# Turning the keys by VectorE and device memory instead of TensorE, in a gated linear attention with a squared-ReLU feed-forward

## The chip, the cores and the metric

One core of one Trainium2 chip runs the whole kernel in one launch. The metric is device time in microseconds (us) of that launch. The kernel before took 495.83 us, the median of three runs (495.6 to 496.37).

## What is computed

All inputs are float32. For 4 sequences (B), 8 heads (H), 768 steps (S) and head dimension 48 (D):

```
f = sigmoid(f_logit)
for t in range(S):
    state = f[:, :, t, :, None] * state + k[:, :, t] (outer) v[:, :, t]
    y[:, :, t] = q[:, :, t] @ state
x = y as [B*S, 384]
out = relu(x @ w_in)**2 @ w_out        # w_in [384, 2048], w_out [2048, 384]
```

The recurrence is a gated linear attention; the feed-forward part holds nearly all the multiplications.

## The kernel before, in words

**Blocks and units.** The 768 steps are cut into 6 blocks of 128 steps (TB). A block of one pair of heads is a *unit*: 24 units, four in each block. A unit works in two chunks of 64 steps (C). Units of head pairs 0 to 2 (`own`) load gates, keys and queries (`fkq`, transposed: head rows on the partitions, 4 x 128 steps along them) and values (`vn`, steps on the partitions). 112 of their 128 rows belong to the pair itself (ROWS); the 16 last rows of either half belong to head pair 3, which has no load of its own: its keys and queries are gathered from the three other units into `last_kq` (stage `m`, L469), its turned keys into `last_kn`.

**The stages of a unit** are letters (L626 to L651): `L` and `v` load; `G` is the sigmoid on ScalarE; `K` (L445) scans the gates on VectorE and multiplies them into the keys (`kt`); `Q` (L458) does the same for the queries; `T` (L494) turns the keys with four 128x128 transposes on TensorE into the PSUM tile `pk`; `N` (L502) copies them on ScalarE to `kn` (steps on the partitions) and to `last_kn`; `D` (L517) multiplies `kn` with the values to the update of the state and `S` the keys with the queries to the scores, both into the PSUM pair `ds`; `M` masks the scores, `C` updates the states, `r` and `s` copy halves, `Y` (L566) computes the outputs, `H` and `X` split them into a high and a low part, the feed-forward's `x`; `h` and `g` send the rows of head pair 3 to the other tiles of `x` by DMA.

**The feed-forward part** works in *rounds*, one for each 128 of the 2048 hidden columns: `up` (9 matmuls of 128x512 into one of two PSUM banks in turn, L247), `square` (ScalarE: relu, square, a copy `gh`, L257 to L259), `rest` (VectorE: `gl`, the remainder, L264), and `down` of the round two earlier (9 matmuls into `po`, L274). The bank of a round is free for the round two later when `rest` has read it. I number the rounds from 0 on: block 1 has rounds 0 to 15, the second half of block 0 has 16 to 23 (its first half is done in an opening part written out by hand, FIRST and SECOND), and blocks 2 to 5 have 24 to 39, 40 to 55, 56 to 71 and 72 to 87. In the first round of a block stands the last `down` of the block before and its output (`finish`, L333, copies and DMAs on SP); the second round of a block has no `down`, so it is only half as long.

**Order.** Every engine works through its instructions in the order in which the program issues them, SP its DMAs too, and a DMA that waits holds up those behind it. Units of blocks 2 to 5 are hung on rounds by hand. Each unit has a *slot*, a round (SLOTS, L63: 12, 14, 18, 20 for block 2; 22, 28, 31, 34 for block 3; 37, 44, 47, 50 for block 4; 53, 60, 63, 66 for block 5; of each four, the last is head pair 3's). In its slot, after `rest`, the stages `Y` of the unit before, then its own `D` and `S`, `H X` of the one before, `r M C`, `m` are issued (L793). Stages ahead of the slot are in STAGE_AT (L60) as (rounds before the slot, place in that round, letters): place 0 is ahead of `up`, 0.5 between `square` and `rest`, 0.7 behind `rest`, 1 behind `down`:

```
STAGE_AT = ((-5, 0, "Lv"), (-3, 1, "GK"), (-2, 0.5, "Q"), (-1, 1, "TN"))
```

So `K` stands at the end of the third round before the slot, `Q` in the next round ahead of its `rest`, and `T` at the end of the round before the slot. `fkq` has a ring of three buffers, `kn` has one.

Of the kernel before, what the change touches and what calls it, by code (L numbers as in the profile page):

```python
# [12 lines left out]
F32 = mybir.dt.float32  # L13
# [10 lines left out]
P = 128  # L24
B, H, S, D = 4, 8, 768, 48
DM, DFF = 384, 2048
HP = H // 2
C = 64
TB = 128
NBLK = S // TB  # L30
NC = TB // C
NT = B * TB
NZ = B * NC
CZ = C + 1
ROWS = 64 + D
# [14 lines left out]
NBUF = 3  # L50
HEADS = 4

# [1 line left out]

STAGE_AT = ((-5, 0, "Lv"), (-3, 1, "GK"), (-2, 0.5, "Q"), (-1, 1, "TN"))  # L60
LAST_AT = ((-5, 0, "v"),)

SLOTS = (12, 14, 18, 20, 22, 28, 31, 34, 37, 44, 47, 50, 53, 60, 63, 66, 69)  # L63
# [297 lines left out]
def fast_path(ctx, tc, moe, ident, low, fkqT, vN, w, w4, out):  # L361
    nc = tc.nc
    V, G = nc.vector, nc.gpsimd
    pers = ctx.enter_context(tc.tile_pool(name="pers", bufs=1))
    dr = pers.tile([P, NZ * CZ], F32, name="dr")
    dz = pers.tile([P, NZ * CZ], F32, name="dz")
    mask = pers.tile([P, C], F32, name="mask")
# [7 lines left out]
    last_kn = pers.tile([P, B, P], F32, name="last_kn")  # L375
# [7 lines left out]
    for r in (0, C):  # L383
        G.affine_select(
            out=mask[r : r + C], in_=mask[r : r + C], compare_op=ALU.is_ge, fill=0.0,
# [12 lines left out]
    def weights_load(f, i, mark=False):  # L398
        raw = moe.words(f, i)
        if mark:  # L400

            V.memset(raw[0:1, 0:1], 0)
        nc.sync.dma_start(raw, w[f, i].bitcast(I16)[:, 1:])

    class Unit:
# [96 lines left out]
        def turned(self):  # L502
# [5 lines left out]
                in_=self.pk.rearrange("p b (h r) -> p b h r", h=2)[:, :, :, D:],  # L508
            )

        @cached_property
        def ds(self):
            return self.pair("ds", -1)
# [112 lines left out]
        def stage(self, letters):  # L626
            for c in letters:
                {
                    "L": lambda: self.load(slice(0, 3)),
                    "f": lambda: self.load(slice(0, 1)),  # L630
                    "p": lambda: self.load(slice(1, 2)),
                    "z": lambda: self.load(slice(2, 3)),
                    "v": lambda: self.load_v(),
                    "G": lambda: self.gates(),
                    "K": lambda: self.keys(),
                    "Q": lambda: self.queries(),
                    "m": lambda: self.move(),
                    "r": lambda: self.crossed(),
                    "T": lambda: self.turn(),
                    "N": lambda: self.turned(),  # L640
                    "D": lambda: self.add(),
                    "S": lambda: self.scores(),
                    "M": lambda: self.masked(),
                    "C": lambda: self.states(),
                    "s": lambda: self.crossed_states(),
                    "Y": lambda: self.outputs(),
                    "H": lambda: self.upper(),
                    "X": lambda: self.lower(),
                    "g": lambda: self.parts((1,), G if self.blk < 2 else nc.sync),
                    "h": lambda: self.parts((0,), nc.sync),  # L650
                }[c]()  # L651
# [73 lines left out]
    with tc.manual_schedule(engines={ET.PE, ET.SP, ET.DVE, ET.Activation, ET.Pool}):  # L725
        with tc.tile_pool(name="ps_p", bufs=2, space=bass.MemoryType.PSUM) as ps_p:
            for t in FIRST.split():
                step(t)
        moe.psum(ctx, "ps_h1", "ps_o")

        moe.sums_of()
        for t in SECOND.split():
            step(t)
        part = []
        owed = moe.ending(lambda po: part.extend(moe.keep(po)))
        whole = half[0] + half[1]
        order = [(1, whole), (0, half[1])] + [(blk, whole) for blk in range(2, NBLK)]
        hooks = [{} for _ in order]

        def hook(k, n, at, do):  # L740
            while n >= len(order[k][1]):
                k, n = k + 1, n - len(order[k][1])
            hooks[k].setdefault((max(n, 0), at), []).append(do)

        def third():
            early.close()
            moe.inputs(ctx)
            xs[2] = moe.new_x(2, 2)

        halves = [(f, i) for f in half[1] for i in range(2)]
        steps = {}

        def advance(h):
            if h not in steps:
                steps[h] = moe.decode(moe.row[halves[h]], lambda: moe.parts(*halves[h]))
            next(steps[h], None)

        for n in range(1, NF - 1):  # L760
            few = range(3 * (n - 1) // 2, min(3 * n // 2, len(halves)))
            for h in few:
                if n < AHEAD:
                    weights_load(*halves[h])
                else:
                    hook(0, n - AHEAD, 0.5, lambda h=h: weights_load(*halves[h], mark=True))

            def before(few=few):
                for h, last in zip(few, (None, *few)):
                    for m in (h, h, last):  # L770
                        if m is not None:
                            advance(m)

            def after(few=few[:-1]):
                for h in few:
                    advance(h)

            def last(few=few):
                for h in few[-1:]:
                    advance(h)  # L780
                    advance(h)


            for place, do in zip((0, 0.5, 0.7) if n > 1 else (0.7, 0.7, 0.7), (before, after, last)):
                hook(0, n, place, do)
        hook(0, 12, 0, third)
        later = [Unit(n, xs, (ps_a,)) for n in range(2 * HP, NBLK * HP)]
        for un, last, at in zip((*later, None), (None, *later), SLOTS):
            if un:
                for n, place, stage in STAGE_AT if un.own else LAST_AT:  # L790
                    hook(0, at + n, place, lambda un=un, stage=stage: un.stage(stage))

            def slot(un=un, last=last):  # L793
                for who, stage in (last, "Y"), (un, "DS"), (last, "HX"), (un, "rMC"), (un, "m" * bool(un and un.own)):
                    if who:
                        who.stage(stage)
                if last and not last.own:
                    last.stage("hg")

            hook(0, at, 0.7, slot)  # L800
            if un:
                hook(0, at + 1, 0, lambda un=un: un.stage("s"))

        for n in range(2 * NF):
            hook(2 + n // NF, n % NF + SIZES_AT, 1, lambda n=n: moe.sizes(n // 2, n % 2))
        general = []
        found = verdict(nc, moe, low, ident, ps_a)
        for n in range(2):
            hook(len(order) - 2, VERDICT_AT + n, 1, lambda: general.append(next(found)))
        hook(  # L810
            len(order) - 1, VERDICT_AT, 1,
            lambda: general.append(nc.values_load(general[1][0:1, 0:1], min_val=0, max_val=1)),
        )
        for k, (blk, fs) in enumerate(order):
            if blk > 1 and blk + 1 < NBLK:
                xs[blk + 1] = moe.new_x(blk + 1, (0, 1, 2)[blk - 2])
            moe.begin(blk, xs[blk], fs)
            if blk == NBLK - 1:

                moe.third_bank = ps_a  # L820
                obs = moe.third_of("ob_last")
                moe.run(hooks[k], obs, owed)
                moe.third_bank = None
            else:
                moe.run(hooks[k], None, owed)
                owed = moe.ending(
                    lambda po, blk=blk: moe.finish(
                        lambda e: out[blk, e * P : (e + 1) * P], None if blk else part, po, blk
                    )
                )  # L830
# [122 lines left out]
@with_exitstack  # L953
def tile_kernel(ctx: ExitStack, tc: tile.TileContext, fkqT, vN, w, w4, out):
    nc = tc.nc
    const = ctx.enter_context(tc.tile_pool(name="const", bufs=1))
    ident = const.tile([P, P], F32, name="ident")
    low = const.tile([P, NBLK * NJ, B * NC], F32, name="low")
    sums = const.tile([P, 2 * NF], F32, name="sums")
    moe = Moe(ctx, tc, const, sums, out)  # L960
    moe.hidden(ctx)
    with ExitStack() as fast:
        rv, obs = fast_path(fast, tc, moe, ident, low, fkqT, vN, w, w4, out)


    with tc.If(rv > 0):
        with ExitStack() as gen:
            general_path(gen, tc, moe, ident, fkqT, vN, w, out)
        for e in range(NJ):
            nc.sync.dma_start(obs[e], out[NBLK - 1, e * P : (e + 1) * P])  # L970

    for e in range(NJ):
        for n, cs in tails(e):

            (nc.sync if n else nc.scalar).dma_start(out[NBLK - 1, e * P : (e + 1) * P, cs], obs[e][:, cs])
# [61 lines left out]
```

## Time and profile before

| | |
|---|---|
| median of three runs | 495.83 us |
| the profiled execution: its time, its span in the trace | 495.6 us, 493.9 us |
| TensorE, granted clock | full speed (0.999) |
| VectorE, ScalarE busy | 48%, 59% of the span |
| DMA: moved, mean rate | 41.96 MB, 85 GB/s |

The span is what the trace covers; 1.7 us of launch lie around it. A row of the trace names the line, the engine, the tiles as out<-in, the count, and then times. PE is TensorE, DVE VectorE, ACT ScalarE, POOL GpSimd, and SP the engine that issues most DMAs.

### The profile page before, as it was taken

Reading aid. Unit: us, or ns where it says so; the run is one execution under the profiler, and the core shown is the slowest. Engines: PE = TensorE matmul, PEld = TensorE weight load, DVE = VectorE, ACT = ScalarE, POOL = GpSimd, SP = SyncE. Lnnn points to the kernel's source line nnn. Section 1 sums busy time; section 2 is a strip of 40 time slices with the busy share of each in tenths; the row PEclk is TensorE's granted clock in tenths of the full one; section 3 lists DMA queues with packets and bytes.
Section 4 is the critical chain, followed back from the end, with each engine's and each line's share of the span. In section 5 each row is a group of like instructions: output and inputs, shape, how many; then the busy total and the mean of one; then the engine's idle time right before and its main releaser. Section 6 shows DMA issues by size and latency. Waiting matters only on the chain.

```text
span 493.9 us, 11450 instructions
## 1 busy us (share of the span) xinstructions
PE 476.2 (96%) x4815; PEld 383.6 (78%) x4815; DVE 237.1 (48%) x444; ACT 292.4 (59%) x615; POOL 29.6 (6%) x66
## 2 busy tenths in 40 slices
PE   3889999999999999999999999999999999999996
PEld 2767777888888888888888888888888877888884
DVE  7999962657654633553632463541563322211112
ACT  5588875977546554656664766664765543544441
POOL 5422010000000000000000000000000000000000
PEclk9999999999999999999999999999999999999999
DMA  8888106570404025330022411014410002100001
GB/s 290 260 290 283 22 20 238 171 264 17 115 3 155 1 40 157 102 90 1 3 44 94 158 30 65 1 17 109 147 26 12 1 1 34 66 0 1 0 1 69
DMA packets 20588, 41.96 MB, mean 85 GB/s; under 512 B 2752, under 2 KB 6192, under 8 KB 20528
## 3 DMA queue, kind: packets, MB, share of 16 engines
q1 hardware_dynamic: 19936, 40.09, 26.1%
q0 software_dynamic: 448, 0.92, 0.9%
q8 instruction: 40, 0.66, 0.5%
q14 instruction: 20, 0.16, 0.1%
q10 hardware_dynamic: 144, 0.13, 0.1%
HBM read 31.68 MB, written 4.72 MB: 74 GB/s over the span
## 4 chain that ended last, share of the span: by engine, by line
PE 92%; DVE 3%; ACT 1%; DMA 1%; issue 1%; POOL 0%; DVEq 0%; ACTq 0%
PE ph L247 41%; PE po L274 41%; PE ds L533 2%; PE ds L522 2%; PE py L581 2%; PE pk L498 1%; PE ph L581 1%; DVE fkq L448 1%; PE py L593 1%; PE ph L593 1%; DMA x<-ys 1%; DMA fkq<-in_fkqT_dram 1%; DVE fkq L462 1%; DVE fkq L454 0%; PE first_py L581 0%
## 5 line engine op out<-in xcount | busy, mean ns | idle before, releaser
L247 PE MATMUL ph<-x,w 128*128 128x512 f32 x864 | 219.1, 399 | 1.3 <-DVE sc L540 1.2
L247 PEld LDWEIGHTS ph<-x,w 128*128 128x128 f32 x864 | 160.8, 188 | 40.4 <-ACT w L143 1.6
L274 PE MATMUL po<-gh,w 128*128 128x512 f32 x576 | 180.9, 395 | 0.0
L264 DVE TENSOR_TENSOR gl<-ph,gh 128x512 fp32r<-128x512 f32 x96 | 66.3, 691 | 235.0 <-ACT gh L259 235.0
L257 ACT ACTIVATE ph<-ph 128x512 f32<-128x512 f32 x96 | 56.0, 583 | 141.3 <-PE ph L247 141.2
L274 PEld LDWEIGHTS po<-gh,w 128*128 128x128 f32 x576 | 108.3, 188 | 25.0
L274 PE MATMUL po<-gl,w 128*128 128x512 f32 x288 | 115.9, 402 | 0.0
L274 PEld LDWEIGHTS po<-gl,w 128*128 128x128 f32 x288 | 54.1, 188 | 14.0 <-DVE gl L264 0.7
L259 ACT CAST gh<-ph 128x512 fp32r<-128x512 f32 x96 | 56.4, 587 | 3.0
L258 ACT ACTIVATE ph<-ph 128x512 f32<-128x512 f32 x96 | 55.9, 582 | 3.0
L453 POOL TENSOR_SCALAR fkq<-fkq 128x8 f32<-128x8 f32 x18 | 12.3, 685 | 302.2 <-DVE fkq L448 104.5
L492 ACT COPY sx<-sp 48x208 f32<-48x208 f32 x44 | 16.0, 365 | 17.1 <-DVE sp L555 16.3
L448 DVE TENSOR_TENSOR_SCAN fkq<-fz,dr 128x520 f32<-128x520 f32 x18 | 22.2, 1234 | 1.8 <-ACT fz L443 1.7
L462 DVE TENSOR_TENSOR_SCAN fkq<-fz,dz 128x520 f32<-128x520 f32 x18 | 22.3, 1242 | 0.6
L581 PEld LDWEIGHTS py<-sc,vn 64*48 64x48 f32 (+1 forms) x384 | 16.4, 126 | 7.4 <-issue 6.6
L498 PE MATMUL pk<-ident,fkq 128*128 128x128 f32 x72 | 12.3, 299 | 9.2 <-POOL fkq L453 6.2
L581 PE MATMUL py<-sc,vn 64*48 64x64 f32 (+1 forms) x384 | 20.9, 222 | 0.0
L131 ACT CAST head<-raw 128x384 f16<-128x384 bf16 (+1 forms) x33 | 19.6, 628 | 0.3 <-DMA raw<-in_w_dram 0.2
L593 PE MATMUL py<-rx,sx 48*48 48x64 f32 x192 | 19.6, 216 | 0.0
L145 DVE TENSOR_TENSOR w<-wa,w 128x384 fp32r<-128x384 f32 (+1 forms) x33 | 18.0, 548 | 2.0 <-ACT w L143 1.5
L143 ACT CAST w<-wa 128x384 fp32r<-128x384 f32 (+1 forms) x33 | 16.5, 510 | 3.6 <-DVE wa L134 3.4
L498 PEld LDWEIGHTS pk<-ident,fkq 128*128 128x128 f32 x72 | 9.5, 153 | 11.4 <-issue 9.1
(102 smaller groups left out, 470.8 us busy)
## 6 DMA issues: line engine op xcount, KB each, us to landing
raw<-in_w_dram SPq DMA_DIRECT2D x32, 383.8 KB, 5.7
fkq<-in_fkqT_dram SPq DMA_DIRECT2D x15, 768.0 KB, 5.0
vn<-in_vN_dram SPq DMA_DIRECT2D x24, 192.0 KB, 4.8
out_dram<-ob SPq DMA_DIRECT2D x12, 256.0 KB, 2.3
fkq<-in_fkqT_dram SPq DMA_DIRECT2D x9, 256.0 KB, 5.0
x<-ys SPq DMA_DIRECT2D x30, 64.0 KB, 2.4
last_kq<-fkq SPq DMA_DIRECT2D x28, 64.5 KB, 2.3
out_dram<-part SPq DMA_DIRECT2D x3, 256.0 KB, 2.1
```

Of the source, the lines that this page charges most:

```text
L131: nc.scalar.copy(out=self.upper(head, F16), in_=high)
L247: self.nc.tensor.matmul(self.ph[f], lhsT=w[:, i], rhs=x[:, j], start=first and n == 0, stop=last and n == 2)
L257: nc.scalar.activation(ph, ph, AF.Relu)
L258: nc.scalar.activation(ph, ph, AF.Square)
L259: nc.scalar.copy(out=gh, in_=ph)
L264: self.nc.vector.tensor_tensor(out=gl, in0=self.ph.pop(f), in1=gh.bitcast(F32), op=ALU.subtract)
L274: self.nc.tensor.matmul(po[e], lhsT=l, rhs=r, start=f == fs[0] and i == 0, stop=f == fs[-1] and i == 2,)
L448: V.tensor_tensor_scan(out=rr[:, ::-1], data0=self.fz[:, NZ * CZ : 0 : -1], data1=dr[:, ::-1], initial=0.0, op0=ALU.mult, op1=ALU.add,)
L462: V.tensor_tensor_scan(out=pp, data0=self.fz[:, : NZ * CZ], data1=dz, initial=0.0, op0=ALU.mult, op1=ALU.add)
L498: nc.tensor.transpose(out=self.pk[:, b], in_=self.kt[:, b * TB : (b + 1) * TB], identity=ident)
L581: nc.tensor.matmul(self.py[c][h * C : h * C + m, b * C : (b + 1) * C], lhsT=self.vn[rows, b, h * D : h * D + m], rhs=self.sc[rows, h, b], ...
L593: nc.tensor.matmul(self.py[c][h * C : h * C + m, b * C : (b + 1) * C], lhsT=s[rows, b * D : b * D + m], rhs=q[rows], start=False, stop=b = ...
```

## The change

In the units of head pairs 0 to 2 of blocks 2 to 5, twelve in all, `T` and `N` are gone. New stages are `t` (`squares`): one VectorE transpose of 32x32 squares, taking every fourth step, into the spent gate rows of the unit's `fkq`, and a DMA of 256 KB to device memory, in which the steps then lie in order; `b` (`back`): four DMAs from there into `kn`, by runs of 32 or 16 floats (128 or 64 bytes); and `l` (`last_back`): two DMAs of 64-byte runs into `last_kn`, in the slot behind `m`. `G`, `K` and `Q` stand one round earlier. The opening part's units keep `T` and `N`. The diff, with blank lines left out:

```
+SQ = 32
-STAGE_AT = ((-5, 0, "Lv"), (-3, 1, "GK"), (-2, 0.5, "Q"), (-1, 1, "TN"))
+STAGE_AT = ((-5, 0, "Lv"), (-4, 1, "GK"), (-3, 0.5, "Q"), (-3, 0.7, "t"), (-2, 1, "b"))
...
+    aside = ctx.enter_context(tc.tile_pool(name="aside", bufs=1, space=bass.MemoryType.DRAM))
...
+        def squares(self):
+            tr = self.rr[:, :NT].rearrange("p (n b d) -> p n b d", b=B, d=SQ)
+            V.transpose(
+                out=tr.rearrange("p n b d -> p b n d"),
+                in_=self.kt.rearrange("p (b t n) -> p b n t", b=B, n=TB // SQ),
+            )
+            self.steps = aside.tile([P // SQ, TB, B, SQ], F32, tag=f"steps{self.nm}", name=f"steps{self.nm}")
+            nc.sync.dma_start(
+                self.steps.rearrange("g (t n) b d -> (g t) (n b d)", t=SQ), tr.rearrange("p n b d -> p (n b d)")
+            )
+        def back(self):
+            self.kn = self.wk([P, B, ROWS], "kn")
+            for g in range(P // SQ):
+                r, m = g * SQ, min(SQ, ROWS - g * SQ)
+                nc.sync.dma_start(self.kn[:, :, r : r + m], self.steps[g, :, :, :m])
+        def last_back(self):
+            for h in range(2):
+                at = h * C + self.hp * (C - D)
+                nc.sync.dma_start(last_kn[:, :, at : at + C - D], self.steps[2 * h + 1, :, :, D - SQ :])
...
+                    "t": lambda: self.squares(),
+                    "b": lambda: self.back(),
+                    "l": lambda: self.last_back(),
...
-                for who, stage in (last, "Y"), (un, "DS"), (last, "HX"), (un, "rMC"), (un, "m" * bool(un and un.own)):
+                for who, stage in (last, "Y"), (un, "DS"), (last, "HX"), (un, "rMC"), (un, "ml" * bool(un and un.own)):
```

## Rows read from the trace of the kernel before

**Rows 1.** The page of the profile: busy time of each engine, and the chain that ended last, its shares by engine.

```profile
PE 476.2 (96%) x4815; PEld 383.6 (78%) x4815; DVE 237.1 (48%) x444; ACT 292.4 (59%) x615; POOL 29.6 (6%) x66
...
PE 92%; DVE 3%; ACT 1%; DMA 1%; issue 1%; POOL 0%; DVEq 0%; ACTq 0%
```

**Rows 2.** The chain that ended last, in order of time, from 160 to 182 us: start, length, engine, tile, line, count. The `up` of rounds 19, 20, 21 and 22 (round 20 is the slot of a unit of head pair 3, without a turn), and the turn at the end of round 21.

```profile
160.33 2.11 PE ph L247 x9
...
164.54 2.10 PE ph L247 x9
...
171.04 2.11 PE ph L247 x9
...
175.24 0.44 PE pk L498 x4
175.68 2.11 PE ph L247 x9
```

**Rows 3.** All that writes or reads the tile `pk`, from 70 us on (the twelve units in question): count, shortest/median/longest in ns, first and last start.

```profile
L498 PE MATMUL pk<-ident,fkq x48: 271/272/273, 123.6 to 373.5; 128*128 128x128 f32 x48
L504 ACT COPY kn<-pk x12: 532/532/539, 124.2 to 373.8; 128x448 f32<-128x448 f32 x12
L506 ACT COPY last_kn<-pk x12: 270/271/281, 124.6 to 374.2; 128x128 f32<-128x128 f32 x12
```

**Rows 4.** The page's costliest groups: two VectorE operations, of 512 and of 384 elements on a partition, with busy time, mean ns of one, and idle time before them.

```profile
L264 DVE TENSOR_TENSOR gl<-ph,gh 128x512 fp32r<-128x512 f32 x96 | 66.3, 691 | 235.0 <-ACT gh L259 235.0
...
L145 DVE TENSOR_TENSOR w<-wa,w 128x384 fp32r<-128x384 f32 (+1 forms) x33 | 18.0, 548 | 2.0 <-ACT w L143 1.5
```

**Rows 5.** VectorE's instructions in order of time in rounds 24 to 26 (start us, length us): the end of block 0 in round 24 (L339), the `rest` of round 25, `K`'s scan (L448), and the `rest` of round 26 behind `K` and `Q`.

```profile
193.00 1.88 DVE L339 TENSOR_TENSOR part<-po,part 128x512 f32<-128x512 f32 x3
196.59 0.69 DVE L264 TENSOR_TENSOR gl<-ph,gh 128x512 fp32r<-128x512 f32 x1 [1.72 <-ACT gh L259]
197.20 1.23 DVE L448 TENSOR_TENSOR_SCAN fkq<-fz,dr 128x520 f32<-128x520 f32 x1
...
201.42 0.68 DVE L264 TENSOR_TENSOR gl<-ph,gh 128x512 fp32r<-128x512 f32 x1
```

**Rows 6.** The chain from 196 to 212 us: the `up` of round 27, and the beginning of `D` in slot 28.

```profile
198.91 2.10 PE ph L247 x9
...
206.74 0.38 PE ds L522 x23
```

**Rows 7.** ScalarE, and below it VectorE, in rounds 40 and 41, the first of block 3 (start, length): the output copies of block 2 (L342), the sigmoid `G` (L443) and the `rest` of round 41.

```profile
269.74 1.08 ACT L342 COPY ob<-po 128x512 f32<-128x512 f32 x2
...
273.94 0.64 ACT L443 ACTIVATE fz<-fkq 128x512 f32<-128x512 f32 x1
...
274.07 0.69 DVE L264 TENSOR_TENSOR gl<-ph,gh 128x512 fp32r<-128x512 f32 x1 [2.91 <-ACT gh L259]
```

**Rows 8.** The page's list of DMAs: KB of one, and the median us from its issue to its landing.

```profile
fkq<-in_fkqT_dram SPq DMA_DIRECT2D x15, 768.0 KB, 5.0
vn<-in_vN_dram SPq DMA_DIRECT2D x24, 192.0 KB, 4.8
out_dram<-ob SPq DMA_DIRECT2D x12, 256.0 KB, 2.3
```

**Rows 9.** DMA packets in three stretches, one queue of each: packets, MB, and the share of 16 engines' time that they took. From 423 to 430 us (7 us; three outputs, together 384 packets of 2 KB and 48 small ones that signal the ends), from 485 to 494 us (9 us; one output on a queue of its own, 128 packets of 1 KB and 16 small ones), and from 80 to 84 us (4 us; weights, 416 packets of 3 KB and 59 small ones).

```profile
q1 hardware_dynamic: 432, 0.79, 29.3%
...
q10 hardware_dynamic: 144, 0.13, 4.9%
...
q1 hardware_dynamic: 475, 1.28, 85.5%
```

**Rows 10.** SP's DMAs in order of time (start, length of the issues, line, out<-in, count): the outputs of block 1 in round 16; the end of block 0 in round 24, and behind it the loads for slot 31; in round 40's place the load for slot 47.

```profile
151.50 1.65 SPq L343 DMA_DIRECT2D out_dram<-ob  x3
...
193.71 1.53 SPq L343 DMA_DIRECT2D out_dram<-part  x3
195.29 0.60 SPq L436 DMA_DIRECT2D fkq<-in_fkqT_dram  x1
195.94 0.62 SPq L440 DMA_DIRECT2D vn<-in_vN_dram  x1
...
272.06 0.61 SPq L436 DMA_DIRECT2D fkq<-in_fkqT_dram  x1
```

**Rows 11.** The chain from 125 to 380 us: where TensorE begins `D` in slots 12, 18, 31 and 44.

```profile
126.28 0.53 PE ds L522 x23
...
157.10 0.35 PE ds L522 x22
...
221.98 0.38 PE ds L522 x22
...
284.22 0.38 PE ds L522 x23
```

**Rows 12.** VectorE in order of time: the `rest` of round 8; the `rest` of round 28; and the end of stage `C` in slot 28.

```profile
110.92 0.69 DVE L264 TENSOR_TENSOR gl<-ph,gh 128x512 fp32r<-128x512 f32 x1 [1.44 <-ACT gh L259]
...
207.53 0.69 DVE L264 TENSOR_TENSOR gl<-ph,gh 128x512 fp32r<-128x512 f32 x1 [3.94 <-ACT gh L259]
...
210.57 0.35 DVE L560 TENSOR_TENSOR state<-sp,ds 112x192 f32<-112x192 f32 x1
```

## The prediction, made before the changed kernel was run

> **What bounds the kernel now.** I read the page's busy times first, then the chain that ended last. TensorE is busy 96% of the span and makes up 92% of the chain [rows 1]; VectorE at 48% and ScalarE at 59% are not the bound. Next I read the chain in order of time, where TensorE's rounds follow each other without a gap. A round without a turn lasts 164.54 - 160.33 = 4.21 us, a round with one 175.68 - 171.04 = 4.64, and the turn's own piece is 0.44 [rows 2]. So whatever leaves TensorE's queue is gained at full length, and whatever makes TensorE wait is lost at full length. The sum has to be made from waits that do not exist yet.
>
> **What is removed.** Twelve turns, 48 transposes [rows 3]: 12 x 0.44 = 5.3 us of the chain. ScalarE loses 24 copies, 12 x (0.53 + 0.27) = 9.6 us [rows 3]; nothing waits for ScalarE on the chain, so I count them as nothing.
>
> **The transpose on VectorE.** The trace has none. Its nearest row is an operation of 512 elements on a partition, 0.69 us; below stands the one of 384 elements, 0.55 [rows 4]; above, twice 0.69, if each square passed twice. I take 0.69 because the count of elements is the same. Twelve are 8 us on an engine that idles half the time; only their place in the way to `kn` matters.
>
> **K and Q one round earlier.** `Q` stands ahead of its round's `rest`, and `up` two rounds later needs the bank that `rest` frees. In a full round that costs nothing: `Q` delays `rest` by some 2 us, and the bank is wanted nearly 4 us after `rest` would end. But for slots 28, 44 and 60 `Q` moves from the third round of a block into the second, which has no `down`. In the kernel before, from the start of `K` to the end of the `rest` behind `Q` are 201.42 + 0.68 - 197.20 = 4.90 us [rows 5]. For slot 28 `K` can now begin when VectorE has finished block 0, at 193.00 + 1.88 = 194.88 [rows 5]; the `rest` of round 25 then ends at 199.78 instead of 197.28, and `up` of round 27 wants to begin at 198.91 [rows 6]: TensorE waits 0.9 us. For slots 44 and 60 `K` waits for ScalarE's two copies and the sigmoid, 269.74 + 1.08 + 0.64 = 271.5 [rows 7], and `rest` ends at 276.4. In round 25 `up` two rounds later came 198.91 - 196.59 = 2.32 us after the start of the old `rest` [rows 5, 6]; here that is 274.07 + 2.32 = 276.4 [rows 7]. Cost 0. Loss by this step: 0.9 us.
>
> **The way to `kn`.** The write is like an output of 256 KB, 2.3 us from issue to landing [rows 8]; `back` may only issue after that. Its four DMAs bring 128 x 4 runs each, 2,048 packets, 128 on each of 16 engines. No packet of data as short as 128 bytes is in the trace. From the shares of engine time, a packet of 2 KB took 0.293 x 16 x 7 us / 384 = 85 ns, one of 1 KB 0.049 x 16 x 9 / 128 = 55, one of 3 KB 0.855 x 16 x 4 / 416 = 132 [rows 9], the small ones counted in. A line through 1 and 2 KB gives 29 ns for 128 bytes; one through 2 and 3 KB falls below the price by bytes alone, 85 / 16 = 5 ns. I take 16, about midway, so 2.05 us for the four DMAs, and keep 5 and 55 (no dearer than 1 KB) as the ends. SP's issue is 0.6 us for each [rows 10], 2.4 for the four.
>
> Three slots have a load queued between write and `back`: the loads for slots 31, 47 and 63 stand behind `t` of slots 28, 44 and 60. Before, they went out at 195.29 and 272.06, as soon as the block's outputs were out [rows 10]; now SP waits at the write for VectorE. Slot 28: the transpose ends at 199.78 + 0.7 = 200.45, SP issues the write (about 0.35) and then the load at 200.8. The load lands 5.0 us later [rows 8], its values some 0.5 behind (8 packets an engine), at 206.3, and the runs for `kn` queue behind them: 208.35. TensorE wants `D` at 206.74 - 0.44 + 0.9 = 207.2 [rows 6]. **Late by 1.15 us.** Slot 44: transpose at 277.05, load at 277.4, `kn` at 277.4 + 5.5 + 2.05 = 284.95, `D` wanted at 284.22 - 0.44 = 283.8 [rows 11]: late by 1.15, and slot 60 is its twin. Slot 18: `back` stands on SP behind block 1's outputs, the last of them issued near 152.8 and landed at 155.1 [rows 8, 10]; `kn` at 157.2, `D` at 157.10 - 0.44 = 156.66 [rows 11]: late by 0.6. Loss: 4.05 us.
>
> The other eight are on time. Slot 31 as an example: `rest` and the slot's own VectorE work end at 210.92 [rows 12]. Even if the later load puts that off to 214.4, the transpose ends at 215.1, the write lands at 217.4, and four issues and a landing of 2.3 end at 221.5; `D`, wanted at 221.98 - 0.44 [rows 11], has by then moved 2 us back by the waits in slot 28. Slot 12: behind the `rest` of round 8 (110.92 [rows 12]) `K`, `Q`, the weights' steps, a `rest` and the transpose take about 7 us, the write lands near 121, `kn` near 125; `D` is wanted at 126.28 - 0.44 [rows 11].
>
> The loads behind `t` also make ScalarE wait for `G` of the next unit, up to 1.7 us (206 against 204); its next work, the square of the slot's round, is not there before 206.5, which hides it. `l` adds 24 issues behind each `m`, needed one slot later, and the sends to the other tiles of `x` follow much later: nothing. The bytes, 12 x 544 KB = 6.5 MB, meet empty queues except where named.
>
> **Sum.** 495.6 - 5.3 + 0.9 + 4.05 = 495.3 us against the profiled execution's own time; the median of the runs stands 0.2 above that, so **495.5 us**. What a measurement of this kernel can tell from no change is about 0.2%, 1 us. One ns more or less for a short packet is 0.128 x 4 = 0.5 us, so the sign hangs on that price.
>
> **Rivals.**
>
> *The short runs are cheap, and the turns are a gain.* At 5 ns for a packet the four DMAs are bound by SP's issues; `kn` of slot 28 is there at 207.0, slots 44 and 60 alike, slot 18 is 0.1 late. Sum 495.6 - 5.3 + 0.9 + 0.1 = 491.3, by the median 491.5; at 10 ns 492.6. For it speaks that one engine's short signalling packets do not show in the 2 KB price; against it the line from 1 KB. [...]
>
> *The return trip becomes the new wait, and the kernel is slower.* Place: the first `D` of slots 18, 28, 44 and 60. It decides from 17 ns a packet on, where the losses eat the 5.3 us. At 29 ns the four DMAs last 3.7 us: slot 18 is 2.1 late, slots 28, 44 and 60 2.8 each, slot 12 about 0.5. Sum 495.6 - 5.3 + 0.9 + 11 = 502.2, by the median 502.4. For it speaks the row of 1 KB; against it that two queues shared the engines there.
>
> *A run below some size costs as a much longer one.* At the line's 40 ns for 512 bytes the DMAs last 5.1 us: four slots about 4 late, slots 12 and 14 about 2 each, three more 0.5: 21 us, 513 us. At 55 ns it is past 525. [...]
>
> A transpose of twice 0.69 us would move slots 28, 44 and 60 by 0.7 each, 2.1 us: inside the forecast's neighbourhood.
>
> **Chances.** Forecast (494.2 to 497.2 its own range) 36%: 22 within 0.2%, 7 on either side. Cheap runs 32%, all faster. Wait at some 29 ns 22%, a dearer run 10%, all slower. So faster 39%, the same 22%, slower 39%. The range leaves out the dear runs and some of either flank: 491.4 to 503.
>
> **What would show it.** `pk` with 24 transposes instead of 72, TensorE's gain 0.44 for each missing one. One VectorE transpose of about 0.7 us in each of twelve units. A wait of `up` for `rest` (L264) of 0.9 us in round 27, none in rounds 43 and 59. Waits of `D` (L522) for the DMAs into `kn`: about 1.15 us in slots 28, 44, 60, 0.6 in slot 18, none elsewhere. Engine time of a packet into `kn` near 16 ns. Wrong would be: no such waits (cheap runs), waits in most of the twelve slots (dear runs), or a wait on another engine that I have hidden, ScalarE's `G` above all.

## The result, and the profile after

The changed kernel takes 500.73 us (median of 4 runs, 500.28 to 501.0) against 495.83 (4 runs, not the three given further up, 495.6 to 496.37): a ratio of 1.0096, with [1.0079, 1.0114] as its 95% interval. The forecast was 495.5, the same; the kernel is slower by 4.9 us, and the interval lies clear of no change. The profiled execution has a span of 498.7 us against 493.9.

The page of the profile after, busy times and the chain by engine:

```profile
PE 475.9 (95%) x4767; PEld 380.6 (76%) x4767; DVE 249.1 (50%) x456; ACT 284.5 (57%) x591; POOL 29.7 (6%) x66
...
PE 78%; DVE 7%; DMA 6%; ACT 4%; issue 2%; SPq 1%; POOL 1%; POOLq 0%; DVEq 0%; ACTq 0%
```

The 48 transposes and 24 copies are gone, as said. What is new stands in the chain: against [rows 1] TensorE fell from 92% to 78%, and VectorE, the DMAs and ScalarE took most of that share. Waits from 72 us on (us in total, times, longest; PEld is TensorE's loading of weights, so one wait can show on both):

```profile
ACT fz L446 <- DMA fkq<-in_fkqT_dram: 11.9, 5, 2.7
...
PEld ph L249 <- DVE x L641: 2.8, 3, 1.1
...
PE ds L548 <- DMA kn<-steps: 2.4, 6, 0.6
PEld ph L249 <- DVE gl L266: 2.0, 3, 1.3
PE ph L249 <- DVE x L641: 1.4, 2, 0.7
...
PE ph L249 <- DVE gl L266: 0.8, 1, 0.8
```

The wait of `up` for `rest` (L266) and that of `D` (L548) for `kn` were forecast. So was ScalarE's `G` (L446) waiting for loads, but as hidden and up to 1.7 us; it came five times, up to 2.7 us (three times behind `t` as named, twice behind the `back` of slots 14 and 18; these two stay in e1 below, where the loss is gone). The wait of `up` (L249) for `X` (L641) was not forecast.

**Where the time goes, round by round.** For each round I take the start of its first `up` matmul in the changed trace less that in the trace of before, and how much this difference grows from the round ahead of it. In rounds that the change doesn't touch it grows by 0.00 to 0.01 us, so small terms can be read. (Executions of one kernel spread by 3 us and more, before as well: 494.8 to 497.8 beside e9. So the mechanisms below are read from rounds, and only the verdicts from the medians. The time ahead of round 0 is not in the table: it differs by -0.62 to +0.87 us between these traces, where the kernels are the same.)

| kernel | a slot's turn gone | 15 | 19 | 27 | 29 | 45 | 61 | all rounds |
|---|---|---|---|---|---|---|---|---|
| after | -0.36 | 0.21 | 1.22 | 0.99 | 1.66 | 1.84 | 1.49 | 4.61 |
| e1 loads first | -0.36 | 0.05 | 1.32 | 0.99 | 0.05 | 0.16 | 0.23 | -0.38 |
| e2 Q behind rest | -0.36 | 0.58 | 1.18 | 0.00 | 1.87 | 3.51 | 1.68 | 5.60 |
| e3 no turn | -0.36 | -0.09 | 0.36 | 0.00 | -0.09 | -0.09 | -0.08 | -4.82 |
| e4 shift alone | 0 | 0.00 | 0.00 | 0.99 | 0.33 | 0.33 | 0.33 | 2.86 |
| e5 all mends | -0.36 | 0.18 | 0.52 | 0.00 | 1.06 | 1.12 | 1.09 | 0.38 |
| e6 back first | -0.36 | 0.08 | 0.43 | 0.99 | 1.52 | 1.94 | 1.80 | 4.16 |
| e7 Q behind slot | -0.36 | 0.28 | 1.42 | 0.99 | 0.95 | 1.06 | 1.14 | 2.81 |
| e8 shift, Q behind | 0 | 0.00 | 0.01 | 0.00 | 0.00 | 0.00 | 0.00 | 0.00 |
| e9 earlier | -0.36 | 0.12 | 1.60 | 0.00 | -0.01 | -0.07 | -0.06 | -1.93 |
| e10 trip for nothing | 0 | 0.00 | 0.91 | 0.00 | 0.00 | 0.00 | 0.00 | 0.80 |
| e11 loads and back | -0.36 | 0.08 | 0.62 | 0.99 | -0.06 | 0.11 | 0.05 | -1.09 |
| e12 slot 18 too | -0.36 | 1.69 | 0.35 | 0.00 | -0.06 | -0.07 | -0.06 | -1.48 |

"All rounds" is the growth from round 0 to round 87. A turn that is gone gives 0.36 ahead of its slot and, in e3, 0.09 more in the round behind the slot: in e3 together the 0.44 of [rows 2]. The five big losses of the changed kernel are those of rounds 19, 27, 29, 45 and 61, 7.2 us together.

**Round 29.** The chain of the changed kernel in order of time, from 196 to 214 us (start, length, what):

```profile
199.36 1.09 DVE fkq L517
...
200.85 5.16 DMA fkq<-in_fkqT_dram
...
206.03 0.64 ACT fz L446
...
206.69 1.25 DVE fkq L451
...
209.03 1.25 DVE fkq L465
...
210.91 0.68 DVE gl L266
211.60 0.34 DVE x L641
...
211.98 2.13 PE ph L249 x8
```

Read it from the end. `up` of round 29 starts when `X` is done, `X` stands on VectorE behind `rest` of slot 28, that behind `Q` and `K` of slot 31's unit, `K` behind `G`, and `G` behind a load that went out at 200.85 instead of 195.29 [rows 10]. Why does `up` need `X`? Because a slot's `Y` borrows the bank of the next round (`spare`), and `X` is what empties it. So the bank of round 29 has two readers ahead of it, and I had looked at `rest` alone. SP's queue at that place, the write, the two loads behind it and `back`:

```profile
200.47 0.33 SPq L522 DMA_DIRECT2D steps<-fkq  x1
200.85 0.61 SPq L439 DMA_DIRECT2D fkq<-in_fkqT_dram  x1
201.51 0.62 SPq L443 DMA_DIRECT2D vn<-in_vN_dram  x1
202.60 2.79 SPq L530 DMA_DIRECT2D kn<-steps  x4
```

That is the queue as forecast (write near 200.45, load at 200.8). From these `back` issues the runs land 3.3, 4.0 and 4.5 us later (shortest, median, longest), behind the loads' bytes (in e1 below, with the loads gone out earlier, 2.6), and `D` waits:

```profile
207.53 0.87 PE L548 MATMUL ds<-vn,kn 64*64 64x48 f32 x30 [0.35 <-DMA kn<-steps]
...
211.98 2.37 PE L249 MATMUL ph<-x,w 128*128 128x512 f32 x9 [0.71 <-DVE x L641]
```

**Price of the pieces.** The transposes, the DMA list (KB of one, median us to landing), and a stretch of 5 us, 325 to 330, in which SP issued only a `back` (packets, MB, share of 16 engines):

```profile
L517 DVE STREAM_TRANSPOSE fkq<-fkq x12: 1078/1098/1104, 117.4 to 371.5; 128x512 f32<-128x512 f32 x12
```

```profile
fkq<-in_fkqT_dram SPq DMA_DIRECT2D x15, 768.0 KB, 5.3
...
steps<-fkq SPq DMA_DIRECT2D x12, 256.0 KB, 2.0
...
kn<-steps SPq DMA_DIRECT2D x36, 64.0 KB, 2.6
```

```profile
q1 hardware_dynamic: 2123, 0.23, 32.5%
```

A short packet took 0.325 x 16 x 5 us / 2,123 = 12.2 ns (a quarter of the runs are of 64 bytes; 2,123 - 2,048 = 75 other packets are counted in, 73 of them under 512 bytes). Forecast: 16, with 5 and 55 as ends.

### The profile page after: what moved, and what is told of

Same layout as the page of the kernel before. It is cut to its first block, busy times and chain, and to the rows that moved or that the text cites. A ratio compares the mean times of both kernels' runs of the same rounds, so it can differ in the third digit from the quotient of the medians.

```text
span 498.7 us, 11446 instructions
## 1 busy us (share of the span) xinstructions
PE 475.9 (95%) x4767; PEld 380.6 (76%) x4767; DVE 249.1 (50%) x456; ACT 284.5 (57%) x591; POOL 29.7 (6%) x66
## 4 chain that ended last, share of the span: by engine, by line
PE 78%; DVE 7%; DMA 6%; ACT 4%; issue 2%; SPq 1%; POOL 1%; POOLq 0%; DVEq 0%; ACTq 0%
PE ph L249 35%; PE po L276 35%; DMA fkq<-in_fkqT_dram 3%; DVE fkq L465 2%; PE ds L559 2%; PE ds L548 2%; DVE fkq L451 2%; PE py L607 1%; DMA kn<-steps 1%; POOL fkq L456 1%; DMA raw<-in_w_dram 1%; PE py L619 1%; PE ph L619 1%; PE ph L607 1%; SPq L530 1%
## 5 line engine op out<-in xcount | busy, mean ns | idle before, releaser
L249 PE MATMUL ph<-x,w 128*128 128x512 f32 x864 | 218.7, 398 | 3.2 <-DVE x L641 1.4
L249 PEld LDWEIGHTS ph<-x,w 128*128 128x128 f32 x864 | 161.2, 188 | 45.4 <-DVE x L641 2.8
L266 DVE TENSOR_TENSOR gl<-ph,gh 128x512 fp32r<-128x512 f32 x96 | 66.1, 689 | 219.0 <-ACT gh L261 215.7
L607 PEld LDWEIGHTS py<-sc,vn 64*48 64x48 f32 (+1 forms) x384 | 16.4, 126 | 7.3 <-issue 7.3
L607 PE MATMUL py<-sc,vn 64*48 64x64 f32 (+1 forms) x384 | 20.9, 222 | 0.0
L446 ACT ACTIVATE fz<-fkq 128x512 f32<-128x512 f32 x18 | 11.4, 635 | 14.4 <-DMA fkq<-in_fkqT_dram 14.4
L548 PE MATMUL ds<-vn,kn 64*64 64x48 f32 (+1 forms) x576 | 15.4, 228 | 3.4 <-DMA kn<-steps 2.4
```

Of the source, the lines that this page charges most:

```text
L249: self.nc.tensor.matmul(self.ph[f], lhsT=w[:, i], rhs=x[:, j], start=first and n == 0, stop=last and n == 2)
L266: self.nc.vector.tensor_tensor(out=gl, in0=self.ph.pop(f), in1=gh.bitcast(F32), op=ALU.subtract)
L548: nc.tensor.matmul(self.ds[h * C : h * C + m, c, b * D : (b + 1) * D], lhsT=self.kn[rows, b, h * C : h * C + m], rhs=self.vn[rows, b, h * ...
L607: nc.tensor.matmul(self.py[c][h * C : h * C + m, b * C : (b + 1) * C], lhsT=self.vn[rows, b, h * D : h * D + m], rhs=self.sc[rows, h, b], ...
```

## The experiments

The edits of e1, e2, e5, e6, e7, e9, e11 and e12 are made to the changed kernel, those of e3, e4, e8 and e10 to the kernel before.

**e1, the loads first.** Slots 31, 47 and 63 load one round earlier, ahead of the wait for the transpose:

```
                 for n, place, stage in STAGE_AT if un.own else LAST_AT:
+                    if stage == "Lv" and at in (31, 47, 63):
+                        n -= 1
```

> The changed kernel, but the loads for slots 31, 47 and 63 are issued one round earlier, so that on SP they stand ahead of the write behind the transpose and not behind it. Theory A (the time is lost in waits made by the order on SP and VectorE): in slots 28, 44 and 60 the next unit's sigmoid, K and Q come on time, the output split X is no longer late, and TensorE's wait of about 1.1 us before the up of rounds 29, 45 and 61 goes, with most of the 0.3 to 0.8 us that D waits for kn there: about 4 us less than the changed kernel, 496.7 us. Theory B (the 37,000 short packets and VectorE's extra work slow everything a little, wherever the loads stand): within 0.5 us of the changed kernel, 500.5 us.

Measured: 495.53 against 495.43, ratio 1.0009 [0.9988, 1.0029]. The edit takes back the whole loss. VectorE and SP of e1 in the same stretch:

```profile
204.34 1.23 DVE L451 TENSOR_TENSOR_SCAN fkq<-fz,dr 128x520 f32<-128x520 f32 x1
...
208.56 0.68 DVE L266 TENSOR_TENSOR gl<-ph,gh 128x512 fp32r<-128x512 f32 x1
209.16 0.41 DVE L641 TENSOR_TENSOR x<-ph,x 112x256 fp32r<-112x256 f32 x1
```

```profile
195.02 0.61 SPq L439 DMA_DIRECT2D fkq<-in_fkqT_dram  x1
195.67 0.62 SPq L443 DMA_DIRECT2D vn<-in_vN_dram  x1
200.44 0.33 SPq L522 DMA_DIRECT2D steps<-fkq  x1
202.52 2.56 SPq L530 DMA_DIRECT2D kn<-steps  x4
```

`K` begins 2.35 us earlier than in the changed kernel, and `X` is done before `up` wants the bank. Only the load was moved, and both waits of rounds 29, 45 and 61 are gone: that for `X`, and that of `D`, which begins at 206.97 with no wait, since the runs now land 2.6 us after their issue (2.2 to 2.7) instead of 4.0. What is left is 0.99 in round 27 and 1.32 in round 19.

**e7, Q behind the slot's work.** In slots 28, 44 and 60 the `Q` of slots 31, 47 and 63 goes behind `rest` and `X`; the loads stay late:

```
+                    if stage == "Q" and at in (31, 47, 63):
+                        place = 0.7
```

> The changed kernel with only this: for slots 31, 47 and 63 Q is issued behind the slot work of slots 28, 44 and 60 and not ahead of it; the loads stay behind the write. If TensorE waits before the up of rounds 29, 45 and 61 because X, which frees the bank that this up needs, stands on VectorE behind the late K and Q: about 0.9 us goes in each of the three, 498 us, and D of slots 31, 47 and 63 is not later. If the loads' bytes ahead of kn in the DMA queues are what costs there: within 0.5 us of the changed kernel, 500.5 us.

Measured: 498.64, ratio 1.0059 [1.0033, 1.0086] (beside 496.09). The waits for `X` are gone; rounds 29, 45 and 61 still lose 0.95, 1.06 and 1.14, and in this kernel `D`'s wait for `kn` is what stands there:

```profile
PE ds L548 <- DMA kn<-steps: 2.5, 4, 0.8
```

So of 4.99 us in these three rounds, 1.84 went with the wait for `X`, and 3.15 is `kn`.

**e4, the shift alone.** The kernel before, turns kept, with `G`, `K` and `Q` one round earlier:

```
-STAGE_AT = ((-5, 0, "Lv"), (-3, 1, "GK"), (-2, 0.5, "Q"), (-1, 1, "TN"))
+STAGE_AT = ((-5, 0, "Lv"), (-4, 1, "GK"), (-3, 0.5, "Q"), (-1, 1, "TN"))
```

> The kernel before with only G, K and Q one round earlier; TensorE's turns stay, nothing goes to device memory. Theory A: the up of round 27 waits about 1.0 us for rest, rounds 43 and 59 0.1 each, the rest is unchanged: 496.8 to 497.1 us. If the shift is harmless and the waits come from the return trip alone: 495.8 us.

Measured: 499.11, ratio 1.0063 [1.0043, 1.0082] (beside 495.43), dearer than expected; 0.87 us of its trace stand ahead of round 0, for no reason that I know. TensorE's waits in it:

```profile
PE ph L247 <- DVE gl L264: 0.8, 1, 0.8
PE ph L247 <- DVE x L615: 0.5, 3, 0.2
```

The first is round 27 as forecast (0.99 by the rounds). The second is the wait for `X`, without any trip to memory: 0.33 in each of rounds 29, 45 and 61, and steps of 0.10 to 0.13 in the rounds beside them, 2.86 us in all. But it is not the changed kernel's wait. Here the loads are on time and `G` is late for another reason: on ScalarE it stands behind `N`'s copies of slot 28, which wait for the turn on TensorE, and the changed kernel has no `N`.

```profile
205.59 0.53 ACT L504 COPY kn<-pk 128x448 f32<-128x448 f32 x1 [0.73 <-PE pk L498]
206.02 0.27 ACT L506 COPY last_kn<-pk 128x128 f32<-128x128 f32 x1
206.17 0.65 ACT L443 ACTIVATE fz<-fkq 128x512 f32<-128x512 f32 x1
```

`G` begins here 0.87 us behind the start of round 28's `up`; in e1, with the changed kernel's loads on time, it begins 0.20 ahead of it, and `X` is done 0.8 us before `up` of round 29 begins.

**e8, the shift with Q behind.** The same, with `Q` behind the slot's work where e4 lost:

```
+                    if stage == "Q" and at in (28, 44, 60, 31, 47, 63):
+                        place = 0.7
```

> The kernel before with G, K and Q one round earlier, as e4_shift_only, but Q behind its round's rest and slot work for slots 28, 44, 60, 31, 47 and 63. If the shift's 2.9 us (the sum over e4's rounds) come from Q standing ahead of rest and X there: 495.6 us, as the kernel before. If they come from K or G or the loads: 498 us or more.

Measured: 496.02, ratio 1.0 [0.9982, 1.0017]. Every step of every round is 0.01 or less. So in the kernel with turns `Q`'s place ahead of `rest` and `X` carries the whole price of the shift.

**e2, Q behind rest everywhere.**

```
-STAGE_AT = (... (-4, 1, "GK"), (-3, 0.5, "Q"), (-3, 0.7, "t"), ...)
+STAGE_AT = (... (-4, 1, "GK"), (-3, 0.7, "Qt"), ...)
```

> The changed kernel, but Q is issued behind its round's rest (and behind the slot's own work, where the round is a slot), right ahead of the transpose. The loads stay where they are. Theory A: the wait before the up of round 27 (1.0 us) goes, rounds 43 and 59 give back 0.1 each, and X in slots 28, 44 and 60 no longer stands behind Q, so the waits of rounds 29, 45 and 61 shrink by about 0.9 each; D's waits for kn stay or grow a little. About 496.8 us. Theory B: within 0.5 us of the changed kernel, 500.5 us.

Measured: 502.33 (499.48 to 505.79), ratio 1.0142 [1.0079, 1.0205]: a miss. Round 27 loses nothing, as expected, but `Q` later makes transpose and write later, and the loads behind the write later still. TensorE's wait in e2:

```profile
PE ds L548 <- DMA kn<-steps: 5.1, 6, 1.5
```

What `Q` no longer holds up, `kn` now does; within these rounds the two can't both be served.

**e3, no turn.** The kernel before without the transposes, with `D` reading the old `last_kn`: it leaves the turning of the keys out, and bounds what the change could gain.

```
-STAGE_AT = (... (-2, 0.5, "Q"), (-1, 1, "TN"))
+STAGE_AT = (... (-2, 0.5, "Q"))
```

> The kernel before without the twelve turns and without anything in their place: G, K and Q stand as before, and D of these units reads last_kn, so the turning of the keys is left out. It measures what TensorE's time for the turns is worth when nothing is put in its place. By the trace, 0.36 us for each turn in the round ahead of the slot (the round's length fell by that in the changed kernel) to 0.44 (the piece of the chain): 490.3 to 491.5 us. If D gives part of it back by waiting for something else that the turn had hidden: 493 us.

Measured: 490.92, ratio 0.9908 [0.9875, 0.9942]. Eleven slots gain 0.44; behind slot 18 round 19 gives back 0.36, a wait of `Y` for `rest` that the turn had covered:

```profile
PE ph L608 <- DVE gl L266: 0.3, 1, 0.3
```

**e6, back first.** `back` ahead of the block's outputs on SP:

```
-STAGE_AT = (... (-2, 1, "b"))
+STAGE_AT = (... (-2, 0.7, "b"))
```

> The changed kernel with only this: back issued at 0.7 of its round, so that for slot 18 it stands ahead of block 1's three outputs on SP. If D of slot 18 waits because the outputs hold up SP: that round's loss of 1.2 us falls to 0.1 or less, 499.5 us. If it waits because the outputs' bytes or the trip itself are slow: no change, 500.7 us.

Measured: 499.94, ratio 1.0093 [1.0056, 1.013]; round 19 falls from 1.22 to 0.43, not to the 0.1 expected. In the changed kernel the chain at slot 18 ran through SP's issues of `back` and the last landing:

```profile
152.61 0.43 SPq L530
...
153.09 0.65 SPq L530
...
153.79 0.62 SPq L530
...
154.46 2.43 DMA kn<-steps
...
157.02 0.56 PE ds L548 x21
```

**e10, the trip for nothing.** The kernel before, turns kept, with the transpose, the write and the two ways back besides, which nobody reads:

```
+STAGE_AT = (... (-2, 0.5, "Q"), (-2, 0.7, "t"), (-1, 1, "bTN"))
```

> The kernel before with the return trip added and not used: TensorE's turns stay and feed D; G, K and Q stand as before; VectorE's transpose runs behind Q's round, the write goes to device memory, and back and last_back bring the same runs, in the same number, into the unit's spent gate rows, which nobody reads. It prices the bytes, the 37,000 short packets, SP's issues and VectorE's 1.1 us each, with nothing waiting for them. Theory A: nothing on TensorE's chain waits, within 0.5 us of the kernel before, 495.8 us. Theory B (short packets slow the other transfers and engines): 2 to 4 us more, 498 to 500 us.

Measured: 497.45, ratio 1.0034 [1.0017, 1.005], between the two expectations. By the rounds the trip costs 0.91 in round 19 and nothing anywhere else; in its profile another 0.67 stands ahead of round 0, where the kernel is the same, so I can't say what it is. Round 19 is SP's queue once more: ScalarE's `CAST` into `gh` waits there 0.94 us for an output to land, because SP sends the outputs at 153.69 instead of 151.50 [rows 10], behind the write of slot 18, which waits for a transpose that ends at 153.29.

```profile
153.31 0.33 SPq L522 DMA_DIRECT2D steps<-fkq  x1
153.69 1.43 SPq L345 DMA_DIRECT2D out_dram<-ob  x3
156.07 0.58 ACT L261 CAST gh<-ph 128x512 fp32r<-128x512 f32 x1 [0.94 <-DMA out_dram<-ob]
```

This place is e10's own: in the changed kernel, which transposes a round earlier, that write goes out at 147.54, ahead of the outputs at 150.76. The trip as such, its bytes and VectorE's 1.1 us, hides.

**e5, all mends.** Loads first, back first, and `Q` behind `rest` both in the second rounds of the blocks and in the slots:

```
+STAGE_AT = (... (-2, 0.7, "b"))
...
+                    if stage == "Lv" and at in (31, 47, 63):
+                        n -= 1
+                    if stage == "Q" and at in (28, 44, 60, 31, 47, 63):
+                        place = 0.7
```

> The changed kernel with three mends of order, nothing added or removed: the loads for slots 31, 47 and 63 one round earlier (ahead of the write on SP), Q behind its round's rest and slot work for slots 28, 44, 60, 31, 47 and 63 only, and back issued at 0.7 of its round, so that for slot 18 it stands ahead of block 1's outputs. Theory A: the turns' gain (e3_no_turn: 4.5 us) stays, less some 0.1 to 0.4 us that D still waits in slots 28, 44 and 60 and 0.1 to 0.2 elsewhere: 492.5 us, 0.6% under the kernel before. Theory B (what is left of the return trip eats the gain whatever the order): 495.4 us, as e1_loads_first.

Measured: 497.93, ratio 1.0044 [1.0022, 1.0067]: a miss, by e2's reason. `Q` behind `rest` in round 25 takes 0.99 from round 27, and puts 1.06 to 1.12 into rounds 29, 45 and 61 as waits of `D`.

**e11, loads and back first**, without moving `Q` (e1 and e6 together).

> e1_loads_first and e6_back_first together: the loads of slots 31, 47 and 63 ahead of the write, back at 0.7. The two mends are of different slots, so they should add: e1's rounds sum to 0.5 us under the kernel before, e6 took 0.8 off slot 18; 1.2 us under the kernel before, 494.4 us. If back at 0.7 only moves the wait on: 495.4 us.

Measured: 495.4 (494.11 to 497.08), ratio 0.9996 [0.9981, 1.001]; by the rounds 1.09 less than before. Not told from no change by the medians.

**e9, a round earlier.** The conflict of e2 and e5 is one of time, so all stages of slots 28, 44 and 60 move one more round forward, out of the second round of their block; with e11's two mends and e7's:

```
+STAGE_AT = (... (-2, 0.7, "b"))
...
+                    if at in (28, 44, 60) or (stage == "Lv" and at in (31, 47, 63)):
+                        n -= 1
+                    if stage == "Q" and at in (31, 47, 63):
+                        place = 0.7
```

> The changed kernel with every stage of slots 28, 44 and 60 one more round earlier (so Q falls into the first round of a block, where VectorE has room ahead of rest), the loads of slots 31, 47 and 63 ahead of the write, their Q behind the slot work, and back at 0.7. Theory A (the losses are places in the order): no wait of up for rest in round 27, no wait of D for kn in slots 28, 44 and 60, slot 18 at 0.4; the turns' gain of 5.3 us less about 2: 3 us under the kernel before, 492.5 us. If the trip has a price of its own that the order does not move: 495 us.

Measured: **493.56** (493.0 to 494.57) against 495.61, ratio 0.995 [0.9931, 0.9969]. It beats both kernels, by less than the 3 us expected. Rounds 27, 29, 45 and 61 lose nothing. What is left is mainly round 19, 1.60 where 0.4 was expected. Its chain, from SP's last `back` issue to TensorE's `Y` (L607):

```profile
151.76 0.63 SPq L530
...
152.49 2.45 DMA out_dram<-ob
...
155.02 0.59 ACT gh L261
...
155.64 0.70 DVE gl L266
...
156.38 0.25 PE ph L607
```

The outputs' tile `ob` is a tile of tag `gh`; ScalarE may fill `gh` again only when the output has landed (its `CAST` waited 1.28 us for that), and the outputs stood behind `back`. So at slot 18 SP's queue costs either way: `back` behind the outputs makes `D` wait, the outputs behind `back` make `rest` late.

**e12, slot 18 too.** To test that, slot 18's stages also go one round earlier, its `Q` behind slot 14's work: `(18, 28, 44, 60)` and `(18, 31, 47, 63)` in e9's two lists.

> The kernel of e9_earlier with slot 18 treated as slots 28, 44 and 60 are: its stages one more round earlier, its Q behind the work of slot 14. Theory: what e9 still loses, 1.6 us at round 19, is one queue. SP issues the outputs of block 1 only behind back of slot 18 (152.49 instead of 150.4), the tile ob of an output is the tile gh of a later round, so ScalarE's CAST into gh waits 1.28 us for the output to land, rest of round 18 comes late and TensorE's Y waits 1.5 us for it. With back of slot 18 issued near 147 the outputs go out as soon as they are copied: no wait of gh for out_dram, round 19 loses at most the 0.36 that it lost without turns, 492.3 us. Rival: the wait comes from VectorE's own order in rounds 15 to 18 or from the slot before it, or Q behind slot 14 makes a new wait; then 493.5 or more.

Measured: 495.85 (494.03 to 497.89), ratio 0.9998 [0.9979, 1.0016]. The mechanism held: `gh` waits for no output, and round 19 loses the 0.35 that it lost in e3. But the loss moved to round 15, 1.69. SP now sends slot 18's loads between the write and `back` of slot 14:

```profile
129.00 0.56 SPq L439
...
129.61 0.62 SPq L443
...
134.97 2.58 DMA kn<-steps
...
137.68 0.56 PE ds L548 x21
```

Here it is less the loads' bytes than their issue on SP: `back` goes out 4.43 us behind the write for 3.16 in e9 (133.01 - 128.58 and 132.08 - 128.92), and the last of it lands the usual 2.6 us after its issue. It is the changed kernel's fault, loads between write and `back`, made again at slot 14. So the rival that was named came true, a new wait elsewhere; e9 stays the best.

## Why the prediction was wrong, step by step

The forecast's sum stood at 495.3 us against a profiled 500.47, 5.2 us short. By the rounds the changed kernel loses 4.61 + 4.82 = 9.43 us against e3; the forecast had 0.9 + 4.05 = 4.95 of it. Of the 4.48 us between, 1.84 are the step that failed, 0.90 small steps of the shift, 1.44 open, and 0.3 slot 18 and round 27. The rest of the 5.2 is mostly the turns: 4.82 us net (e3) for 5.3, since slot 18 gains nothing.

**Right.** The turns (0.44 each in eleven of twelve slots, e3). The wait in round 27: 0.99 for 0.9; 0.10 and 0.11 in rounds 43 and 59 for 0. The late `kn` in slots 28, 44 and 60, its cause (loads queued behind `t`, shown by e1) and its size: by e7, against e3's rounds, 1.04, 1.15 and 1.22 for 1.15 each. That the size fits so well is partly luck, as two of its terms were off in opposite directions (below). The short packet: 12.2 ns for 16, so the dear runs at 29 ns and the run that costs like a much longer one, 40 ns, are out. (The 512 bytes that the 40 ns are read at were my assumption; no row or run shows such a size.)

**The step that failed** is the one on the loads: "its next work, the square of the slot's round, is not there before 206.5, which hides it". ScalarE stood 2.30 us before `G` in round 28, and I had followed its own next work and not what waits for `G`'s result. That is `K` and `Q` on VectorE, and behind them `rest` and `X`. The prediction even put VectorE's work of slot 28 off, from 210.92 to 214.4, and asked this of slot 31's `kn` alone. With it fell "In a full round that costs nothing": for slots 28, 44 and 60 that round holds an `X` too, and the bank it frees is wanted by the very next `up`, not two rounds later. I had counted the bank's use by `rest` and not the one that `Y` makes by `spare`. Price: 1.84 us (after less e7). It takes both, a late `G` and `Q` ahead of `X`: with the loads on time the wait is gone though `Q` stays where it is (e1), with `Q` behind `X` it is gone though the loads stay late (e7). The same late loads delayed `kn`, as forecast.

**Mis-sized.** Beside those steps the shift also costs 0.10 to 0.13 in each of rounds 28, 30, 43, 44, 46, 59, 60 and 62 (43 and 59 are those named above): 0.90 us in after less e3, there in e4, gone in e8. Slot 18 came out at 1.22 for 0.6 (its own numbers give 157.2 - 156.66 = 0.54): 0.36 of it is a wait that the turn had covered (e3). The transpose takes 1.10 us for 0.69; the 0.4 it adds to the way to `kn` was about what the cheaper packets gave back (128 x 4 ns = 0.5 us).

**Open.** Behind nearly every slot `up` comes 0.1 to 0.2 us later than in e3 (round 23: +0.05 for -0.09), 1.4 us over all slots. Each time `D` reads what DMAs wrote instead of what ScalarE copied. It is no wait for the trip: in slot 22 the last of `kn` landed at 174.07 and `D` began at 178.31. And it is not the DMAs' traffic, for e10 has that and loses nothing there. The time lies in `D`'s own stretch on TensorE: from the last start of `Y` to the last of `S` slot 22 takes 1.07 us, 0.93 before and in e3. What it is, no run shows.

**The rivals.** "The return trip becomes the new wait, and the kernel is slower" gave the sign and nearly the time (502.4), at the four places that it named; but its price, 29 ns a packet, was not what decided. The trip alone, run beside the turns with nobody reading it, costs 0.91 us in one place (e10), by the order on SP there. The order on SP's and VectorE's queues cost most of the rest, as e9 shows, which pays the same packets and is faster than before.

## What to carry to other kernels

When a step moves to another place in an in-order queue, list everything behind it in that queue, and for each buffer that work frees, every user of it, the borrowed uses too. A producer that waits must not stand ahead of independent loads: sending three loads one round earlier was worth 5 us (e1). And a trip through memory takes some 7.6 us here from the start of the transpose to the first `D` (199.34 to 206.97 in slot 28 of e1, where `D` does not wait, and the last run landed at 207.03). In slots 28, 44 and 60 it had to start one more round ahead (e9); in the rounds it had, one wait was only traded for another (e2, e5).

## What the runs showed of the hardware that was not expected

VectorE's transpose of 32 x 32 squares, 512 elements of f32 on a partition, took 1.10 us, while a two-input operation of as many elements takes 0.69 [rows 4]. 2,048 runs of 64 and 128 bytes, read from device memory, cost 12.2 ns of engine time each, far below 55 for a packet of 1 KB [rows 9]; SP's issue, 0.63 us for each of four, was longer than the time that one of them keeps the 16 engines busy, by an estimate from the 12.2 ns: 512 x 12.2 ns / 16 = 0.4 us. And the same four DMAs landed 2.6 us after issue with no load ahead of them (e1, slot 28) and 4.0 behind loads of 768 and 192 KB (the changed kernel).
